# First four attention units: probabilities turned by a product with diagonals of reciprocals, and a product over zeros ahead of each group of turns

## The chip, the cores and the metric

The kernel runs on one core of one Trainium2 chip. The metric is the time of one execution on the device in microseconds (us), lower is better. TensorE (PE) multiplies matrices, VectorE (DVE) and ScalarE (ACT) work on vectors, GpSimd (POOL) does slower vector work, and SyncE (SP) issues most DMAs. Each engine works through its own queue in order; an instruction that waits holds up everything behind it on that engine.

## The reference

Three stages follow one another: attention with a causal mask and a bias from cumulated gates, then two MLP layers.

```python
B, H, S, D = 4, 8, 576, 64
cum = np.cumsum(np.maximum(s, 0.0), axis=-1)
bias = np.minimum(-(cum[..., :, None] - cum[..., None, :]), 0.0)
scores = np.where(causal, -1e9, q @ k.T / 8 + bias)
attn = np.exp(scores - scores.max(-1))
attn = attn / (attn.sum(-1) + 1e-9)
x = (attn @ v)                      # -> 2304 x 512
h = x @ w_in; r = np.maximum(h, 0)  # 512 -> 2048
x = (s * r * r + b) @ w_out         # 2048 -> 512
h = x @ w_in2; g = np.maximum(h, 0) + alpha * np.minimum(h, 0)
x = g @ w_out2
```

## The kernel before

Attention is cut into 32 **units**: a batch, a pair of heads, and a range of query rows. Units 0 to 3 are the four pairs of heads of batch 0, each with query rows 0 to 319 in blocks of 64, 128 and 128 rows. Only after all four does the first token block of the MLP have all of its 512 inputs, so the first MLP product, `hp` on L781, stands behind them. From there on `attention()` yields single steps of the later units in between MLP products, and PE has work of one kind while the other waits.

For one head of a unit, `scores` writes the bias (L433 on DVE for the first head, L429 on ACT for the second), multiplies q and k on PE (L455), adds bias and product and keeps the row's extreme on DVE (L459), takes the exponential with the row's sum on ACT (L471), adds 1e-9 to the sums and takes reciprocals on DVE (L478, L479), and multiplies each block by its reciprocals on POOL (L482). Then `values` turns the blocks on PE into a bank `pt` (L513: six 128x128 turns a head in two banks, each a transpose against the identity), copies the bank to `pf` (L517, ACT for the first bank, DVE for the second), multiplies with v into `av` (L529), and copies the result out (L544).

Besides, the first MLP weights are unpacked: for each half of a packet, `convert` does one pass on ACT (L140) and two on DVE (L141, L142) into `wt_<packet>_<half>`, half 0 from `wi` and half 1 from `wo`; then L130 and L131 split it. The q and k of a unit come by DMA into `nat` and are turned on DVE (L373) into `turned`. `busy(n)` (L97) multiplies zeros into a scratch bank n times on PE; 16 run at the start, and single ones stand between the steps of the first four units.

The code is written per unit, but the order on each engine's queue is set at build time by a scheduler, which moves instructions by its own estimate of when each could start; only `busy` is held in program order. Any change of instructions can therefore move others.

In names such as `probs_0_2_0_508` the parts are batch, pair of heads and range and then a buffer number, and printed names lose digits directly behind letters: `sc_1_0_0_2_0` is the score of block 1 of unit 2, `nm_2_0_1` and `sm_2_0_1` belong to unit 2 (pair 2, range 0), second head. `turned_0_1` and `nat_0_1` are unit 4's (pair 0, range 1), the first that isn't one of the first four.

Of the kernel before, what the change touches and what calls it, by code (L numbers as in the profile page):

```python
# [8 lines left out]
F32 = mybir.dt.float32  # L9
# [4 lines left out]
ALU = mybir.AluOpType  # L14
# [5 lines left out]
def tile_forget_attention__then__two_mlps(  # L20
# [20 lines left out]
    nc = tc.nc  # L41
    B, H, S, D = q.shape
    NT, DM = out.shape
    DFF = w_in1.shape[1] // 2
    P = 128
    NP = H // 2
# [5 lines left out]
    IB = [(0, 64)] + [(64 + 128 * n, 192 + 128 * n) for n in range(4)]  # L52
    R1 = IB[2][1]
    QK = S - R1 + S
    EARLY, NATIVE = NP, 2 * NP

# [8 lines left out]
    one = ctx.enter_context(tc.tile_pool(name="one", bufs=1))  # L67
# [12 lines left out]
    ident = const.tile([P, P], F32, name="ident")  # L80
# [13 lines left out]
    def busy(n):  # L94

        for _ in range(n):
            tc.keep_in_program_order(nc.tensor.matmul(scratch, dense[:, :P], dense, start=True, stop=True))  # L97
# [31 lines left out]
    def split(hi, lo, src, lo_eng=nc.vector):  # L129
        nc.scalar.copy(hi, src)  # L130
        lo_eng.tensor_tensor(out=lo, in0=src, in1=hi.bitcast(F32), op=ALU.subtract)  # L131
# [36 lines left out]
    for f in range(len(SPARE), NF):  # L168
        at = int((f - len(SPARE)) * PACE)
# [106 lines left out]
    class Unit:  # L276
        def __init__(self, n):
            self.n = n
            self.b, self.pr, self.rng = units[n]
            self.tag = "_".join(str(i) for i in units[n])  # L280
            self.h0 = 2 * self.pr
            self.blocks = (0, 1, 2) if self.rng == 0 else (3, 4)
            self.q0, self.q1 = (0, R1) if self.rng == 0 else (R1, S)
            self.nv = 3 if self.rng == 0 else 4
            self.probs = [None, None]

            self.early = 0 < n < EARLY
            self.native = n < NATIVE
            self.n_banks = 0
            self.cums = []  # L290

# [110 lines left out]
    def scores(u, h):  # L402

        own = HALF[h]
        head = u.b * H + u.h0 + h
        flip = u.native and h == 1
        nr = len(u.blocks)
        nm = two.tile([P, 3], F32, tag="nm", name=f"nm_{u.tag}_{h}")
        sm = two.tile([P, 3], F32, tag="sm", name=f"sm_{u.tag}_{h}")
        if u.rng == 0:  # L410
            nc.gpsimd.memset(sm[:, 0:1], 1.0)
        big = None if u.early else two.tile([P, 1088], F32, tag="probs", name=f"probs_{u.tag}_{h}")
        probs, col = {}, 0
        for r in u.blocks:
            i0, i1 = IB[r]
            rows = i1 - i0
            if u.early and r != 1:
                big, col = u.buf(two, 0, F32, "", f"probs{h}{r}"), 0

            width = -(-i1 // P) * P if i1 < S else S  # L420
            pt = probs[r] = big[:, col : col + width]
            col += width
            if width > i1:
                nc.gpsimd.memset(pt[:, i1:], 0.0)
            if r == 0:
                nc.gpsimd.memset(pt[64:P, 0:64], 0.0)

            if flip:
                nc.scalar.activation(  # L429
                    pt[:rows, :i1], u.cums[h][:rows, :i1], AF.Relu, scale=-1.0, bias=cumT[:rows, r, head : head + 1]  # L430
                )
            else:
                nc.vector.tensor_scalar(  # L433
                    out=pt[:rows, :i1], in0=u.cums[h][:rows, :i1], scalar1=cumT[:rows, r, head : head + 1],
                    scalar2=0.0, op0=ALU.subtract, op1=ALU.min,
                )
            nc.gpsimd.affine_select(
                out=pt[:rows, i0:i1], in_=pt[:rows, i0:i1], pattern=[[-1, rows]], base=0,
                channel_multiplier=1, compare_op=ALU.is_ge,
                fill=-MASKED if flip else MASKED,  # L440
            )
        u.probs[h] = probs
        for m, r in enumerate(u.blocks):
            i0, i1 = IB[r]
            rows, n = i1 - i0, i1
            a0 = i0 - u.q0
            pt = probs[r]
            init = -KEEP_ALL if flip else KEEP_ALL
            for j0, j1 in ([(0, n)] if n <= 512 else [(0, 320), (320, n)]):
                sc = u.bank("sc", f"sc{h}_{r}_{j0}")  # L450

                scr, all_ = sc[:rows, : j1 - j0], sc[:, : j1 - j0]
                aq = slice(a0, a0 + P)
                if u.native:
                    nc.tensor.matmul(all_, u.qk[0][own, aq], u.qk[1][own, j0:j1], start=True, stop=True)  # L455
                else:
                    nc.tensor.matmul(all_, u.xs[h][0][:, aq], u.xs[h][1][:, j0:j1], start=True, stop=False)
                    nc.tensor.matmul(all_, u.ql[h][:, aq], u.xs[h][1][:, j0:j1], start=False, stop=True)  # L458
                nc.vector.tensor_tensor_reduce(  # L459
                    out=pt[:rows, j0:j1], in0=scr, in1=pt[:rows, j0:j1], scale=SCALE if flip else -SCALE, scalar=init,  # L460
                    op0=ALU.subtract if flip else ALU.add, op1=ALU.max if flip else ALU.min,
                    accum_out=nm[:rows, m : m + 1],
                )
                if u.n < EARLY:
                    busy(1)
                init = nm[:rows, m : m + 1]
            if flip:
                nc.vector.tensor_scalar(
                    out=nm[:rows, m : m + 1], in0=nm[:rows, m : m + 1], scalar1=-1.0, scalar2=None, op0=ALU.mult
                )  # L470
            nc.scalar.activation(  # L471
                pt[:rows, :n], pt[:rows, :n], AF.Exp, bias=nm[:rows, m : m + 1], scale=1.0 if flip else -1.0,
                accum_out=sm[:rows, m : m + 1],
            )
            yield
        if u.n == 0:
            busy(4)
        nc.vector.tensor_scalar(out=sm[:, :nr], in0=sm[:, :nr], scalar1=1e-9, scalar2=None, op0=ALU.add)  # L478
        nc.vector.reciprocal(sm[:, :nr], sm[:, :nr])  # L479
        for m, r in enumerate(u.blocks):  # L480
            rows, n = IB[r][1] - IB[r][0], IB[r][1]
            nc.gpsimd.tensor_scalar(  # L482
                out=probs[r][:rows, :n], in0=probs[r][:rows, :n], scalar1=sm[:rows, m : m + 1],
                scalar2=1.0, op0=ALU.mult, op1=ALU.mult,
            )
        yield

    def values(u, h):
# [10 lines left out]
        for n_bank, bank in enumerate(banks):  # L499
            f0, fn = bank[0][1], bank[-1][1] + width[bank[-1][0]]  # L500
            tp = u.bank("tr", f"pt{h}_{n_bank}")
            moves = []
            for c, off in bank:
                for r in u.blocks:
                    i0, i1 = IB[r]
                    if P * c >= i1:
                        continue

                    partial = r and P * c > i0
                    o = off + i0 - max(q0, P * c)  # L510
                    moves.append((not partial, -c if partial else o, o, r, min(P * c, S - P)))
            for _, _, o, r, k0 in sorted(moves):
                nc.tensor.transpose(tp[:, o : o + P], u.probs[h][r][:, k0 : k0 + P], ident)  # L513
            n_p = (2 * h + n_bank) % 2
            if u.native:
                pf = two.tile([P, 512], F32, tag=("ph", "pl")[n_p], name=f"pf_{u.tag}_{h}_{n_bank}")
                (nc.scalar.copy, nc.vector.tensor_copy)[n_p](pf[:, f0:fn], tp[:, f0:fn])  # L517
                parts = (pf,)
            else:
                ph = two.tile([P, 512], F32R, tag="ph", name=f"ph_{u.tag}_{h}_{n_bank}")  # L520
                pl = two.tile([P, 512], F32R, tag="pl", name=f"pl_{u.tag}_{h}_{n_bank}")
                split(ph[:, f0:fn], pl[:, f0:fn], tp[:, f0:fn])
                parts = (ph, pl)
            yield
            for z, part in enumerate(parts):
                for c, o in bank:
                    w = width[c]
                    lhs = (u.vn if u.native else u.vs[h])[:, c].rearrange("p z d -> p (z d)")
                    nc.tensor.matmul(  # L529
                        av[:, nq - w : nq], lhs, part[:, o : o + w],  # L530
                        start=(c == 0 and z == 0), stop=(c == last_c and z == len(parts) - 1),
                        skip_group_check=True,
                    )
# [451 lines left out]
    for n in range(len(BLOCKS) * NF):  # L985
# [20 lines left out]
        for j in range(NF):  # L1006
            at = LAG[0] + int((j - len(SPARE)) * PACE) if j >= len(SPARE) else j
# [46 lines left out]
```

## Time and profile before

| | |
|---|---|
| Median of three runs | 1039.33 us (1038.52 to 1040.82) |
| Profiled execution, its own time | 1039.36 us |
| Its span, first to last instruction | 1037.6 us |
| PE busy | 98% of the span |
| DVE / ACT / POOL busy | 65% / 65% / 43% |
| Mean granted TensorE clock | 0.996 |

The span is what the engines' records cover; 1.8 us of the execution lie around it. A row of the timeline tells when an instruction, or a run of like ones, began, how long it took, and in square brackets how long the engine had been idle before and what ended that. Grouped rows give count, busy time and mean.

### The profile page before, as it was taken

How to read it: one execution, taken by the hardware profiler on the slowest of the kernel's cores; microseconds unless marked ns; L12 is line 12 of the kernel's file. 1: busy time of each engine (PE TensorE's matmuls, PEld its weight loads, DVE VectorE, ACT ScalarE, POOL GpSimd, SP SyncE). 2: the span in 40 equal slices, each digit the busy share in tenths (PEclk: the TensorE clock that was granted, in tenths of full speed). 3: DMA queues.
4: the chain of work that ended last, by engine and by line, in shares of the span. 5: the costliest groups of instructions: out<-in, count | busy, mean ns of one | idle time of the engine just before them, and what ended most of it. 6: DMA issues, size and time to landing. Idle time of an engine off the chain costs nothing. (4 is left out here: it accounts for less than half of the span.)

```text
span 1037.6 us, 20643 instructions
## 1 busy us (share of the span) xinstructions
PE 1018.5 (98%) x6949; PEld 925.5 (89%) x6952; DVE 674.4 (65%) x1605; ACT 670.7 (65%) x1668; POOL 450.6 (43%) x876
## 2 busy tenths in 40 slices
PE   9999999999999999999999999999999999999997
PEld 4578899999999999999999888888999999999996
DVE  6899665687677766677655865857665456455443
ACT  5878766777787877878776776645554454445433
POOL 5555675666677576777562000574611011001000
PEclk9899999999999999999999999999999999999999
DMA  7997443343143432324215762645644335334331
GB/s 150 257 249 223 120 76 68 73 98 76 40 89 67 99 72 52 82 65 91 68 34 177 230 199 78 205 148 176 200 154 142 102 114 171 103 102 133 105 102 48
DMA packets 197930, 125.45 MB, mean 121 GB/s; under 512 B 138496, under 2 KB 167936, under 8 KB 197824
## 3 DMA queue, kind: packets, MB, share of 16 engines
q1 hardware_dynamic: 193744, 123.56, 42.8%
q8 instruction: 55, 0.90, 0.4%
q10 hardware_dynamic: 4080, 0.57, 0.3%
q14 instruction: 51, 0.42, 0.1%
HBM read 106.19 MB, written 17.90 MB: 120 GB/s over the span
## 5 line engine op out<-in xcount | busy, mean ns | idle before, releaser
L781 PE MATMUL hp<-xh,w 128*128 128x256 f32 (+1 forms) x1024 | 229.9, 301 | 1.1 <-ACT r L800 1.1
L905 PE MATMUL acc<-w,ring 128*128 128x512 f32 x864 | 214.6, 392 | 1.1 <-DVE ring L131 0.7
L905 PEld LDWEIGHTS acc<-w,ring 128*128 128x128 f32 x864 | 155.9, 188 | 29.4 <-DVE ring L131 1.1
L781 PEld LDWEIGHTS hp<-xh,w 128*128 128x128 f32 x1024 | 171.4, 189 | 9.3 <-ACT r L800 1.4
L895 PE MATMUL acc<-gh,w 128*128 128x256 f32 x896 | 170.3, 286 | 0.4 <-ACT res L924 0.4
L781 PE MATMUL hp<-xl,w 128*128 128x256 f32 (+1 forms) x512 | 152.3, 298 | 0.0
L895 PEld LDWEIGHTS acc<-gh,w 128*128 128x128 f32 x896 | 135.3, 189 | 2.4 <-ACT res L924 1.0
L881 POOL TENSOR_TENSOR cc<-u,t 128x256 f32<-128x256 f32 x32 | 26.9, 839 | 237.2 <-DVE u L872 202.9
L895 PE MATMUL acc<-gl,w 128*128 128x256 f32 x448 | 117.7, 288 | 1.4 <-POOL gl L131 1.4
L482 POOL TENSOR_SCALAR probs<-probs,sm 64x64 f32<-64x64 f32 (+4 forms) x160 | 89.2, 571 | 58.9 <-DVE sm L479 51.9
L471 ACT ACTIVATE probs<-probs,nm 64x64 f32<-64x64 f32 (+4 forms) x160 | 89.9, 562 | 35.8 <-DVE nm L459 26.9
L131 POOL TENSOR_TENSOR gl<-r,gh 128x256 fp32r<-128x256 f32 x112 | 87.7, 784 | 51.3 <-ACT gh L130 41.4
L815 PE MATMUL p<-xs,sums 128*128 128x256 f32 x768 | 104.6, 282 | 0.4 <-DVE u L857 0.4
L815 PEld LDWEIGHTS p<-xs,sums 128*128 128x128 f32 x768 | 98.0, 189 | 2.0 <-DVE u L857 0.6
L781 PEld LDWEIGHTS hp<-xl,w 128*128 128x128 f32 x512 | 97.1, 190 | 2.7
L459 DVE CUSTOM_DVE_ANT_0 probs<-sc,probs 128x320 f32<-128x320 f32 (+3 forms) x160 | 68.4, 428 | 42.1 <-PE sc L458 28.8
L815 PEld LDWEIGHTS p<-xs,w 128*128 128x128 f32 x576 | 79.0, 189 | 8.4 <-DVE u L872 1.7
L800 ACT ACTIVATE r<-hp 128x256 f32<-128x256 f32 (+1 forms) x144 | 58.0, 403 | 43.7 <-PE hp L781 31.6
L815 PE MATMUL p<-xs,w 128*128 128x256 f32 x576 | 82.0, 282 | 2.3 <-DVE u L872 1.5
L895 PEld LDWEIGHTS acc<-gl,w 128*128 128x128 f32 x448 | 79.8, 189 | 2.5 <-POOL gl L131 1.9
L513 PE MATMUL pt<-ident,probs 128*128 128x128 f32 x480 | 75.3, 275 | 3.1 <-POOL probs L482 2.7
L826 DVE SCALAR_TENSOR_TENSOR ph<-pl,misc,ph 128x512 f32<-128x512 f32 x64 | 50.6, 790 | 42.3 <-ACT pl L842 42.3
(151 smaller groups left out, 2104.3 us busy)
## 6 DMA issues: line engine op xcount, KB each, us to landing
sums<-sums_d SPq DMA_DIRECT2D x128, 256.0 KB, 2.7
wi<-in_moe_w_in_dram SPq DMA_DIRECT2D x32, 512.0 KB, 5.0
wo<-in_moe_w_out_dram SPq DMA_DIRECT2D x32, 512.0 KB, 5.1
cum<-cum_d SPq DMA_DIRECT2D x32, 288.0 KB, 3.6
sums_d<-w SPq DMA_DIRECT2D x64, 128.0 KB, 1.9
cum<-cum_d SPq DMA_DIRECT2D x30, 160.0 KB, 3.0
nat<-in_k_dram SPq DMA_DIRECT2D x64, 72.0 KB, 2.5
x_d<-res SPq DMA_DIRECT2D x18, 256.0 KB, 2.4
```

The lines of the kernel that those rows point to most:

```text
L131: lo_eng.tensor_tensor(out=lo, in0=src, in1=hi.bitcast(F32), op=ALU.subtract)
L459: nc.vector.tensor_tensor_reduce(out=pt[:rows, j0:j1], in0=scr, in1=pt[:rows, j0:j1], scale=SCALE if flip else -SCALE, scalar=init, op0=AL ...
L471: nc.scalar.activation(pt[:rows, :n], pt[:rows, :n], AF.Exp, bias=nm[:rows, m : m + 1], scale=1.0 if flip else -1.0, accum_out=sm[:rows, m ...
L482: nc.gpsimd.tensor_scalar(out=probs[r][:rows, :n], in0=probs[r][:rows, :n], scalar1=sm[:rows, m : m + 1], scalar2=1.0, op0=ALU.mult, op1=A ...
L513: nc.tensor.transpose(tp[:, o : o + P], u.probs[h][r][:, k0 : k0 + P], ident)
L781: nc.tensor.matmul(hs, a[:, c], b[c], start=(n == 0), stop=(n == len(terms) * NCC - 1))
L800: relus.append(nc.scalar.activation(r, hs, AF.Relu, scale=1.0 / W_SCALE).ins)
L815: nc.tensor.matmul(bank, lhs[:, c * P : (c + 1) * P], rhs[:, c], start=(start and c == 0 and z == 0), stop=(c == 1 and z == 2), skip_group ...
L826: nc.vector.scalar_tensor_tensor(out=r, in0=u, scalar=nalpha[:, f : f + 1], in1=r, op0=ALU.mult, op1=ALU.add).ins
L881: nc.gpsimd.tensor_tensor(out=cc[:, T:], in0=u3, in1=t5, op=ALU.add)
L895: nc.tensor.matmul(banks[d] if count == 2 else acc[d // 2][:, d % 2], a[:, d * P : (d + 1) * P], b, start=(f == 0 and (d % 2 == 0 or count ...
L905: nc.tensor.matmul(banks[m], a[:, m * P : (m + 1) * P], b, start=(f == 0 and b is woh and a is gh), stop=(f == NF - 1 and a is gl),)
```

## The change

For units 0 to 3 (`SPREAD = 4`) the 24 multiplies on POOL (three a head) are gone. In their place DVE multiplies the identity by the reciprocals, block by block, into a tile `diag` (tags xs0 and xs1): a diagonal matrix of 64x64, 128x128 and 128x128 per head. A turn is no longer a transpose against the identity but a product of the block with its diagonal, which turns and scales at once; it is a product in fp32, and masked columns (`skip`) are left out, so three turns a head have 64 columns and three have 128. Eight memsets of 64x64 on POOL go, and one `busy(1)` is added ahead of each group of turns: two banks, two heads, four units, so 16.

```diff
-    EARLY, NATIVE = NP, 2 * NP
+    EARLY, NATIVE, SPREAD = NP, 2 * NP, 4
...
-            if r == 0:
+            if r == 0 and not u.spread:
                 nc.gpsimd.memset(pt[64:P, 0:64], 0.0)
...
         nc.vector.reciprocal(sm[:, :nr], sm[:, :nr])
+        if u.spread:
+            u.diag[h] = one.tile([P, QK], F32, tag=f"xs{h}", name=f"diag{h}_{u.tag}")
         for m, r in enumerate(u.blocks):
             rows, n = IB[r][1] - IB[r][0], IB[r][1]
+            if u.spread:
+                turn = u.diag[h][:rows, m * P : m * P + rows]
+                nc.vector.tensor_scalar(
+                    out=turn, in0=ident[:rows, :rows], scalar1=sm[:rows, m : m + 1], scalar2=None, op0=ALU.mult
+                )
+                continue
             nc.gpsimd.tensor_scalar(
...
             tp = u.bank("tr", f"pt{h}_{n_bank}")
             moves = []
+            if u.n < EARLY:
+                busy(1)
...
-                    moves.append((not partial, -c if partial else o, o, r, min(P * c, S - P)))
-            for _, _, o, r, k0 in sorted(moves):
+                    moves.append((not partial, -c if partial else o, o, r, min(P * c, S - P), max(0, P * c - i0)))
+            for _, _, o, r, k0, skip in sorted(moves):
+                if u.spread:
+                    rows = IB[r][1] - IB[r][0]
+                    at = (r - u.blocks[0]) * P
+                    nc.tensor.matmul(
+                        tp[:, o + skip : o + rows], u.probs[h][r][:rows, k0 : k0 + P],
+                        u.diag[h][:rows, at + skip : at + rows], start=True, stop=True,
+                    )
+                    continue
                 nc.tensor.transpose(tp[:, o : o + P], u.probs[h][r][:, k0 : k0 + P], ident)
```

In the changed kernel the new multiply is L488, the new turn L528, and the old turn L533; L455, L459, L373, L517, L529 and L781 are L457, L461, L375, L537, L549 and L801.

The scheduler's order moves with it. The queue of SP's DMAs keeps its order, and from the first MLP products on, PE's keeps it too.

On DVE, where unit 2 scores its first head, `sc_1_0_0_2_0` is block 1 and `sc_2_0_0_2_0` block 2. Before:

```order
L459 ISA probs_0_2_0_508,nm_2_0_0_505<-sc_1_0_0_2_0_539,probs_0_2_0_508 128x192
L459 ISA nm_2_0_0_505 128x1
L141 TENSOR_SCALAR wt_1_0_226<-wt_1_0_226 128x512
L459 ISA probs_0_2_0_520,nm_2_0_0_505<-sc_2_0_0_2_0_550,probs_0_2_0_520 128x320
L459 ISA nm_2_0_0_505 128x1
L142 SCALAR_TENSOR_TENSOR wt_1_0_226<-wi_1_216,wt_1_0_226 128x512
```

After:

```order
L141 TENSOR_SCALAR wt_2_0_246<-wt_2_0_246 128x512
L142 SCALAR_TENSOR_TENSOR wt_2_0_246<-wi_2_242,wt_2_0_246 128x512
L141 TENSOR_SCALAR wt_2_1_250<-wt_2_1_250 128x512
L461 ISA probs_0_2_0_512,nm_2_0_0_509<-sc_1_0_0_2_0_543,probs_0_2_0_512 128x192
L461 ISA nm_2_0_0_509 128x1
L142 SCALAR_TENSOR_TENSOR wt_2_1_250<-wo_2_243,wt_2_1_250 128x512
```

The unpacking of packets 1 and 2, which stood behind this score, now stands ahead of it; in the same way block 1 of the second head now stands behind `wt_3_0` and `wt_3_1`.

On DVE, at the turn of unit 4's q and k (`turned_0_1`). Before:

```order
L459 ISA probs_0_3_0_737,nm_3_0_1_722<-sc_2_0_0_3_0_770,probs_0_3_0_737 128x320
L459 ISA nm_3_0_1_722 128x1
L142 SCALAR_TENSOR_TENSOR wt_3_1_649<-wo_3_263,wt_3_1_649 128x512
L468 TENSOR_SCALAR nm_3_0_1_722<-nm_3_0_1_722 128x1
L131 TENSOR_TENSOR xl_0_870<-xf_433,xh_0_869 128x256
L373 STREAM_TRANSPOSE turned_0_1_695<-nat_0_1_564 128x832
```

After:

```order
L461 ISA probs_0_3_0_672,nm_3_0_0_669<-sc_0_0_0_3_0_689,probs_0_3_0_672 64x64
L461 ISA nm_3_0_0_669 64x1
L470 TENSOR_SCALAR nm_2_0_1_588<-nm_2_0_1_588 128x1
L375 STREAM_TRANSPOSE turned_0_1_703<-nat_0_1_570 128x832
L480 TENSOR_SCALAR sm_2_0_1_589<-sm_2_0_1_589 128x3
L435 TENSOR_SCALAR probs_0_1_0_831<-cum_0_0_1_579,cumT 128x448
L537 COPY pf_2_0_0_1_715<-pt_1_0_2_0_712 128x64
L435 TENSOR_SCALAR probs_0_1_0_831<-cum_0_0_1_579,cumT 128x576
L481 RECIPROCAL sm_2_0_1_589<-sm_2_0_1_589 128x3
L461 ISA probs_0_3_0_672,nm_3_0_0_669<-sc_1_0_0_3_0_705,probs_0_3_0_672 128x192
```

It stood behind the last score of unit 3's second head; now it stands behind the first score of unit 3's first head, with the other five scores of unit 3 behind it.

On PE, the last rows ahead of the first MLP product. Before:

```order
L513 MATMUL pt_0_0_3_0_832<-ident,probs_0_3_0_737 128x128 x2
L513 MATMUL pt_1_0_3_0_849<-ident,probs_0_3_0_737 128x128
L455 MATMUL sc_3_0_0_0_1_934<-turned_0_1_695 128x448
L529 MATMUL av_0_3_0_831<-pf_3_0_1_0_838,vn_3_0_223 128x320
L529 MATMUL av_0_3_0_831<-pf_3_0_1_0_838,vn_3_0_223 128x192
L529 MATMUL av_0_3_0_831<-pf_3_0_1_1_851,vn_3_0_223 128x64
L97 LDWEIGHTS dense
L97 MATMUL acc_first_96<-dense 128x512
L781 MATMUL hp_0_0_881<-xh_0_869,w_0_0_0_204 128x256
```

After:

```order
L528 MATMUL pt_0_0_3_0_846<-diag_0_3_0_793,probs_0_3_0_735 128x64 x2
L528 MATMUL pt_0_0_3_0_846<-diag_0_3_0_793,probs_0_3_0_735 128x128
L528 MATMUL pt_0_0_3_0_846<-diag_0_3_0_793,probs_0_3_0_746 128x128 x2
L549 MATMUL av_0_3_0_845<-pf_3_0_1_0_853,vn_3_0_223 128x320
L549 MATMUL av_0_3_0_845<-pf_3_0_1_0_853,vn_3_0_223 128x192
L97 LDWEIGHTS dense
L97 MATMUL acc_first_96<-dense 128x512
L549 MATMUL av_0_3_0_845<-pf_3_0_1_1_867,vn_3_0_223 128x64
L97 LDWEIGHTS dense
L97 MATMUL acc_first_96<-dense 128x512
L801 MATMUL hp_0_0_897<-xh_0_885,w_0_0_0_204 128x256
```

The same first MLP product stands at the end of both; the score `sc_3_0_0_0_1` of unit 4 moved ahead of this group of turns, and a product over zeros came in.

## Rows read from the trace of the kernel before

**Rows 1.** The page: the span, and the engines' busy time, share, instructions.

```profile
span 1037.6 us, 20643 instructions
PE 1018.5 (98%) x6949; PEld 925.5 (89%) x6952; DVE 674.4 (65%) x1605; ACT 670.7 (65%) x1668; POOL 450.6 (43%) x876
```

**Rows 2.** By stretch: length, busy us and count per engine, granted clock, DMA share.

```profile
0.00:60.00 60.00, 54.13 (x227) 30.74 (x230) 46.38 (x154) 40.55 (x117) 34.53 (x113) 0.94 0.86 208
38.00:42.00 4.00, 4.00 (x11) 2.42 (x10) 3.62 (x14) 3.40 (x11) 0.23 (x1) 0.50 0.48 107
48.00:55.00 7.00, 5.64 (x29) 4.06 (x30) 6.97 (x16) 4.91 (x13) 5.04 (x10) 1.00 1.05 334
60.00:120.00 60.00, 59.68 (x392) 50.10 (x391) 53.23 (x112) 49.03 (x119) 35.30 (x52) 1.00 0.80 219
```

**Rows 3.** Timeline of DVE: start, duration, instruction [idle before <-releaser].

```profile
22.48 0.39 DVE L141 TENSOR_SCALAR wt<-wt 128x512 uint32<-128x512 uint32 x1
29.05 0.34 DVE L459 CUSTOM_DVE_ANT_0 probs<-sc,probs 128x192 f32<-128x192 f32 x1
33.14 0.91 DVE L141 TENSOR_SCALAR wt<-wt 128x512 uint32<-128x512 uint32 x1 [0.68 <-ACT wt L140]
48.66 1.03 DVE L373 STREAM_TRANSPOSE turned<-nat 128x832 f32<-128x832 f32 x1
```

**Rows 4.** DMA of wo, packet 2, issued at 29.2 (SP).

```profile
L212 SPq DMA_DIRECT2D wo<-in_moe_w_out_dram x1: 1804/1804/1804, 29.2 to 29.2; - x1
DMA to landing us min/median/max: 7.7/7.7/7.7
```

**Rows 5.** DMA of wo, packet 3, issued at 31.6 (SP).

```profile
L212 SPq DMA_DIRECT2D wo<-in_moe_w_out_dram x1: 503/503/503, 31.6 to 31.6; - x1
DMA to landing us min/median/max: 8.2/8.2/8.2
```

**Rows 6.** DMAs of unit 4's k into nat, issued up to 44.5 (SP).

```profile
L325 SPq DMA_DIRECT2D nat<-in_k_dram x3: 311/496/1033, 42.6 to 44.5; - x3
DMA to landing us min/median/max: 2.9/3.8/3.8
```

**Rows 7.** Timeline of PE.

```profile
15.90 0.82 PE L513 MATMUL pt<-ident,probs 128*128 128x128 f32 x6
33.30 1.06 PE L513 MATMUL pt<-ident,probs 128*128 128x128 f32 x6 [0.70 <-POOL probs L482]
49.97 0.49 PE L513 MATMUL pt<-ident,probs 128*128 128x128 f32 x3
50.39 1.99 PE L455 MATMUL sc<-turned 64*128 64x448 f32 x6
53.79 1.20 PE L529 MATMUL acc_first<-pf,vn 128*128 128x320 f32 x6
54.82 1.03 PE L97 MATMUL acc_first<-dense 128*128 128x512 bf16 x4
58.68 0.47 PE L781 MATMUL hp<-xh,w 128*128 128x256 f32 x1
```

**Rows 8.** Timeline of POOL, the multiplies of one head.

```profile
32.54 1.22 POOL L482 TENSOR_SCALAR probs<-probs,sm 64x64 f32<-64x64 f32 x3 [2.53 <-DVE nm L468]
```

**Rows 9.** Groups of DVE by shape, 8 to 60 us: busy us, mean ns, idle before.

```profile
L459 DVE CUSTOM_DVE_ANT_0 probs<-sc,probs 128x320 f32<-128x320 f32 x9 | 4.3, 476 | 1.0 <-PE sc L455 1.0
L141 DVE TENSOR_SCALAR wt<-wt 128x512 uint32<-128x512 uint32 x8 | 4.3, 535 | 1.9 <-ACT wt L140 1.9
L479 DVE RECIPROCAL sm<-sm 128x3 f32<-128x3 f32 x8 | 1.3, 159 | 0.1
L433 DVE TENSOR_SCALAR probs<-cum,cumT 128x448 f32<-128x448 f32 x1 | 0.4, 437 | 0.0
```

**Rows 10.** Groups of ACT by shape, 8 to 60 us.

```profile
L471 ACT ACTIVATE probs<-probs,nm 128x320 f32<-128x320 f32 x8 | 4.4, 550 | 0.3 <-DVE nm L459 0.3
L471 ACT ACTIVATION_READ_ACCUMULATOR probs<-probs,nm 128x1 f32 x19 | 3.6, 187 | 0.0
```

More of the change, by code (lines that the diff above doesn't have):

```diff
@@ L288, in __init__ @@
             self.native = n < NATIVE
+            self.spread = n < SPREAD
+            self.diag = [None, None]
             self.n_banks = 0
```

## Prediction

> **What bounds the kernel now.** I read the page first: PE is busy for 1018.5 of 1037.6 us [rows 1]. With 2% idle, the question is where the idle time lies, and the stretches answer it. In the first 60 us PE is busy for 54.13, and its clock is 0.94 on average; from 60 to 120 it idles for 0.3 us in all [rows 2]. So from the first MLP product, which starts at 58.68 [rows 7], PE is a queue that is never empty, and whatever delays that product delays all that follows; whatever brings it forward brings the end forward. The case is decided by one number: when that product starts.
>
> Next I read the timeline backwards from it. In 48 to 55 us DVE is busy for 6.97 of 7.00 us and PE for 5.64 [rows 2]: PE waits for what the vector engines hand over. In that stretch DVE turns unit 4's q and k at 48.66 [rows 3]. Their last load is issued at 44.5 and takes up to 3.8 us [rows 6], so it lands near 48.3, and DVE takes it up almost at once. Before the change all scores of units 2 and 3 are behind DVE by then, and 10.0 us later (58.68 less 48.66) the first MLP product starts.
>
> **The change part by part.** *POOL.* The multiplies of one head take 1.22 us in the row that shows three together [rows 8], eight heads some 10 us, all of it gone. POOL is off the chain except where a turn waits for it, as at 33.30 for 0.70 us [rows 7]. The eight memsets I cost at nothing, because the 16 products over zeros at the start cover them; without that cover each is smaller than one of the three multiplies (0.4), so 3.2 in all is their upper bound, as a gain.
>
> *DVE.* Three diagonals a head come in. The trace shows no such row. From below, the reciprocal of 3 columns takes 0.159; from above, a shift of 512 columns 0.39 undisturbed [rows 3, 9]. On the line between the two, 64 columns cost 0.19 and 128 columns 0.22, which makes 0.62 a head and 5.0 for eight (bounds 3.8 and 9.4). I take 5.0, since the sizes lie near the lower end.
>
> In return DVE may run faster. A shift of L141 takes 0.39 at 22.48, but 0.91 at 33.14 while POOL multiplies from 32.54 to 33.76 [rows 3, 8]; the mean of eight is 0.535 [rows 9], so their loss is 8 x 0.145 = 1.2 us, and as much again for the eight passes of L142 (an estimate from the same rows): up to 2.4 back, not all of it owed to these multiplies. The Trainium skill, "SBUF — State Buffer", section "SBUF: two separate sides", states that VectorE in its faster modes and GpSimd take turns at a shared pair of ports, and that the loser is blocked for the whole instruction; the trace agrees with 0.39 against 0.91. By that rule alone, taking POOL's multiplies away speaks for the change, and all of the 2.4 would come back.
>
> *PE.* Six turns in a row take 0.82 and three 0.49, so a turn costs 0.11 [rows 7]. The new turn is an fp32 product as L455 is: 1024 columns in two passes each take 1.99 less about 0.27 of tail, or 0.84 ns a column and pass, so 128 columns take 0.215. For 64 columns I take the same, because the 128 rows of the block must be loaded in any case (lower bound 0.11). That is +0.63 a head, 5.0 for eight (bounds 2.5 and 5.0). A product over zeros costs about 0.215 (four in 1.03 with the next row 0.86 later [rows 7]): 16 cost 3.4. All this matters only where PE isn't waiting; in the first 60 us it idles 5.9 us [rows 2].
>
> *The order.* This term decides. As the queue of the DMAs does not change, unit 4's loads land near 48.3 whatever the engines do. But DVE's queue has changed in two places.
>
> First, block 1 of unit 2's first head, scored at 29.05 before [rows 3], now stands behind the shift of `wt_2_1`, which needs `wo` of packet 2; that landed at 29.2 + 7.7 = 36.9 [rows 4]. Block 1 of its second head stands behind `wt_3_1`, which needs 31.6 + 8.2 = 39.8 [rows 5] and then ACT's and DVE's passes, so about 42. Behind the waiting shift in DVE's queue stand all further scores, and behind those PE's turns and `av`. So heads that were finished at 29 to 46 us are done 8 us later and more, and DVE reaches the turn of unit 4 with five scores of unit 3 undone.
>
> Second, that turn now stands ahead of those five scores, and waits for the load. I start it at 48.66, as before. Then on DVE, one after another: the turn 1.03; sums of unit 2's second head 0.16; bias of 448 columns 0.44; a copy 0.20; bias of 576 columns 0.56 (0.437 x 576/448); reciprocal 0.16; score of block 1 0.34 and its read-out 0.08 [rows 3, 9]; a split `xl` 0.40 and the copy's 0.20 as estimates near the bias row; three diagonals 0.62; score of block 2 0.48 and read-out 0.08. Together 4.55. Then ACT's exponential with its read-out 0.55 + 0.19 = 0.74 [rows 10], sums and reciprocal 0.32, a score that stands between 0.42, two diagonals 0.41 and a handoff of 0.1: 1.99. PE gets the diagonals of unit 3's first head at 48.66 + 4.55 + 1.99 = 55.2.
>
> From there PE has, in its new order up to the first MLP product: 12 turns x 0.215 = 2.6; scores of unit 4, 448 + 320 + 256 + 448 columns in two passes at 0.84 ns = 2.5; three groups of `av` at 1.03 = 3.1 (the group at 53.79 is followed at 54.82 [rows 7]); 12 products over zeros x 0.215 = 2.6; and one wait for ACT's copy of a bank, some 0.8 by the row of 0.55. Sum 11.6, so the product starts at **66.8** instead of 58.68, +8.1 us. Working it with the bounds of turn (64 columns at 0.11: -0.6) and diagonal (0.48 to 1.17 a head: -0.2 to +0.9) and the load 0.4 earlier gives +7 to +9.
>
> *What is given back later.* PE's order does not change afterwards, and it idles 0.3 us in 60 to 120, while DVE is busy for 53.23 of 60 [rows 2], and stays as late as PE makes it. I take nothing, and bound it at 3 us, for weights that would be waited for less. The sum: 1039.36 + 8.1 = 1047.5, and as the profiled execution lies on the median (1039.33), 1047.4.
>
> **The rivals.** *Faster.* The order is harmless, because DVE and PE arrive earlier than the weights' DMAs let me assume. Then each head's own chain is shorter by 1.22 - 0.62 = 0.6 on its last step, and the 2.4 of slowed DVE passes come back in the stretch where DVE is busy throughout: 1039.3 - 3.0 = 1036.3. For it: PE's waits ahead of turns are for POOL [rows 7]. Against it: the fp32 turns and zeros add 8.4 us to PE against 5.9 idle, and the scores do stand behind the weights in the queue. The rule of the page cited above is the one that would carry this. Chance 0.14.
>
> *No change.* DVE is never long without work, so what it does in another order adds up to the same; then +5.0 for diagonals, -2.4 for undisturbed passes and -2 to -3 of DVE's waits filled gives 1039 to 1040. Against it: in an in-order queue the waits at `wt_2_1` and `wt_3_1` are not filled. Chance 0.10.
>
> *Slower still.* The clock falls in the new gap. Before, it stands at 0.50 from 38 to 42 us [rows 2], which is the 1.2 of the two levels of 1.2 and 2.4 GHz; the mean of 0.94 over 60 us means some 7 us at half. With PE waiting more in 42 to 55, as much of that may fall on the 11.6 us of PE's own chain, where it costs half of 7.2, 3.6 us: 1051. The zeros ahead of the turns speak against it, as they are queued behind the same waits. Chance 0.15.
>
> *That the change doesn't do what it says* would be a turn that still waits as long for DVE's diagonals as for POOL; this is part of my likeliest case and needs no price of its own.
>
> **How the numbers follow.** About 0.2%, or 2 us, is what a measurement of this kernel can tell from no change. Likeliest, with 0.61: +8.1, 1047.4, between 1044.5 (3 us given back) and 1048.5. With 0.15 about 1051, with 0.10 about 1039.5, with 0.14 about 1036.3. The range from 1039 to 1052 leaves out the faster rival and little else. Faster 0.14, same 0.10, slower 0.61 + 0.15 = 0.76.
>
> **What would show it.** After the change, the first MLP product near 66.8 us, later ones all 7 to 9 us late with the same spacing; unit 2's block 1 scored after 37 us on DVE with a long wait on the `wt` shifts ahead of it; PE idle for some 8 to 12 us more in the first 60; L141 without values near 0.9 where POOL multiplied. Step by step: diagonals at 0.19 to 0.22, new turns 0.215 apart, zeros 0.215 each. I am wrong if the first MLP product starts before 60 us: then the scores did not wait for the weights as their order says, or the zeros and fp32 turns were idle time. I am also wrong if it starts late but the delay melts away before 300 us; then PE's full share hid waits that the records count as work.

## The result and the profile after

The changed kernel took 1047.49 us (median of six runs, 1046.51 to 1049.31) against 1040.39 for the kernel before in the same session, a ratio of 1.0081 with an interval from 1.0065 to 1.0097. It is slower by about 8 us.

The runs of one kernel differ in how long TensorE's clock stands at half, so a few comparisons below name the mean granted clock. At 0.995 to 0.997, eight runs of the changed kernel from all sessions have a median of 1046.56 and 29 runs of the kernel before 1038.49: 8.1 us.

The page of the changed kernel, from a run of 1049.31 us at a clock of 0.991 (span and busy time, to be held against [rows 1]):

```profile
span 1047.5 us, 20756 instructions
PE 1031.1 (98%) x7012; PEld 934.9 (89%) x7016; DVE 674.0 (64%) x1629; ACT 671.7 (64%) x1668; POOL 437.9 (42%) x844
```

Its stretches, as in [rows 2]:

```profile
0.00:60.00 60.00, 56.55 (x234) 32.37 (x237) 42.48 (x157) 35.43 (x101) 20.75 (x78) 0.86 0.84 205
60.00:120.00 60.00, 59.27 (x377) 48.53 (x377) 50.36 (x119) 47.74 (x116) 31.10 (x45) 1.00 0.69 192
```

PE is busier in the first 60 us (56.55 against 54.13), DVE less busy (42.48 against 46.38) and POOL much less (20.75 against 34.53). The clock is 0.86 there against 0.94, and the first MLP product, at 58.68 before, starts at 70.22. That run isn't on the clock of the profile before, so the readings below come from a later run of the same kernel that is (`after_third`, 1046.57 us at 0.996). The same stretch there, and the DVE and PE timelines around unit 4's turn:

```profile
0.00:60.00 60.00, 54.13 (x247) 32.40 (x251) 44.71 (x167) 37.15 (x107) 20.85 (x78) 0.94 0.86 206
44.00:65.00 21.00, 20.64 (x104) 13.62 (x106) 14.79 (x63) 14.07 (x42) 3.79 (x8) 1.00 0.99 247
```

```profile
47.41 1.05 DVE L375 STREAM_TRANSPOSE turned<-nat 128x832 f32<-128x832 f32 x1 [1.65 <-DMA nat<-in_k_dram]
...
49.27 0.45 DVE L435 TENSOR_SCALAR probs<-cum,cumT 128x448 f32<-128x448 f32 x1 [0.77 <-DMA cum<-cum_d]
...
53.41 0.63 DVE L488 TENSOR_SCALAR diag<-ident,sm 64x64 f32<-64x64 f32 x3
```

```profile
44.30 1.80 PE L528 MATMUL pt<-diag,probs 128*128 128x64 f32 x12 [1.08 <-DVE diag L488]
...
51.63 1.73 PE L528 MATMUL pt<-diag,probs 128*128 128x64 f32 x12
53.28 0.80 PE L457 MATMUL sc<-turnedk,turnedq 64*128 64x320 f32 x2
54.02 1.66 PE L528 MATMUL pt<-diag,probs 128*128 128x64 f32 x10
55.61 1.55 PE L457 MATMUL sc<-turned 64*128 64x448 f32 x4
...
63.72 1.56 PE L528 MATMUL pt<-diag,probs 128*128 128x64 f32 x10
65.95 1.13 PE L549 MATMUL av<-pf,vn 128*128 128x320 f32 x4 [0.68 <-ACT pf L537]
...
67.33 0.47 PE L801 MATMUL hp<-xh,w 128*128 128x256 f32 x1
```

Up to the first MLP product PE's time is, in the kernel before and then in `after_third`:

```profile
0.00:58.68 58.68, 52.81 (x217) 29.47 (x221) 46.00 (x152) 39.43 (x113) 33.21 (x111) 0.94 0.87 210
0.00:67.33 67.33, 60.79 (x280) 37.02 (x285) 48.10 (x178) 40.55 (x115) 23.46 (x81) 0.95 0.84 208
```

At an equal clock the first MLP product starts at 67.33 against 58.68 [rows 7], 8.6 us later. The turn of unit 4 does wait for its load, 1.65 us, with DVE's queue behind it, and the diagonals of unit 3's first head are done at 53.41 + 0.56 = 53.97 (the next DVE instruction starts then). PE takes them up at 54.02. But PE came to that place without a gap: from 44.3 on it has no wait of its own until 65.95. DVE's late diagonals and PE's longer queue arrive at the same moment. Of the 8.6 us PE is busy for 8.0 (60.79 less 52.81) and idle for 0.7 (6.54 less 5.87): the loss is work that the old waits did not hide. Whether the new order kept those waits from being filled, or the work alone makes the loss, the trace can't say by itself.

### The profile page after: what moved, and what is told of

It is laid out like the page before. It is cut to its first block, busy times and chain, and to the rows that moved or that the text cites. A ratio compares the mean times of both kernels' runs of the same rounds, so it can differ in the third digit from the quotient of the medians.

```text
span 1047.5 us, 20756 instructions
## 1 busy us (share of the span) xinstructions
PE 1031.1 (98%) x7012; PEld 934.9 (89%) x7016; DVE 674.0 (64%) x1629; ACT 671.7 (64%) x1668; POOL 437.9 (42%) x844
## 5 line engine op out<-in xcount | busy, mean ns | idle before, releaser
L801 PE MATMUL hp<-xh,w 128*128 128x256 f32 (+1 forms) x1024 | 229.9, 301 | 1.1 <-ACT r L820 1.1
L801 PEld LDWEIGHTS hp<-xh,w 128*128 128x128 f32 x1024 | 171.4, 189 | 9.4 <-ACT r L820 1.5
L801 PE MATMUL hp<-xl,w 128*128 128x256 f32 (+1 forms) x512 | 152.3, 298 | 0.0
L461 DVE CUSTOM_DVE_ANT_0 probs<-sc,probs 128x320 f32<-128x320 f32 (+3 forms) x160 | 68.3, 428 | 49.6 <-PE sc L460 28.5
L801 PEld LDWEIGHTS hp<-xl,w 128*128 128x128 f32 x512 | 97.1, 190 | 2.7
L492 POOL TENSOR_SCALAR probs<-probs,sm 128x448 f32<-128x448 f32 (+4 forms) x136 | 77.1, 580 | 40.3 <-DVE sm L481 39.3
L567 DVE TENSOR_TENSOR xf<-av,xf 64x128 f32<-64x128 f32 (+3 forms) x88 | 28.0, 319 | 69.4 <-ACT xf L566 68.9
```

The lines of the kernel that those rows point to most:

```text
L461: nc.vector.tensor_tensor_reduce(out=pt[:rows, j0:j1], in0=scr, in1=pt[:rows, j0:j1], scale=SCALE if flip else -SCALE, scalar=init, op0=AL ...
L492: nc.gpsimd.tensor_scalar(out=probs[r][:rows, :n], in0=probs[r][:rows, :n], scalar1=sm[:rows, m : m + 1], scalar2=1.0, op0=ALU.mult, op1=A ...
L567: nc.vector.tensor_tensor(out=dst, in0=src, in1=dst, op=ALU.add)
L801: nc.tensor.matmul(hs, a[:, c], b[c], start=(n == 0), stop=(n == len(terms) * NCC - 1))
```

## The experiments

The theories: **order** (DVE's new order delays the first four units, as predicted), **work** (PE simply has more to do, with fp32 turns and zeros), and **clock** (the half-clock stretch became longer). Each kernel's first MLP product is given beside its time, since the first 60 us can be read there free of what later units do. The queues are held by `issue_after`, which puts instructions behind a given one on the same engine.

### The changed kernel again: `after_again`, `after_third`, `after_fourth`

> The changed kernel once more, for a second profile. Its first profile granted 0.86 of the clock in the first 60 us and had PE busy without a gap from 38 to 68 us. Order theory (DVE's queue delays units 2 and 3 behind the weights and unit 4's loads): with more clock PE idles 4 us or more in 36 to 60, and the first MLP product still starts near 66 to 68 us. Work theory (PE has about 8.4 us more to do, the fp32 turns and the zeros): PE stays busy without gaps there and the first product comes near 67 to 70. Clock theory (the longer stretch at half clock makes the loss): the first product comes before 63 us where the clock is not lower than in the kernel before.

> The changed kernel for another profile, wanted at a mean clock near 0.996 as in four of its ten runs so far. Theory that PE's own added work bounds the first 60 us: PE without gaps over 0.3 us from 36 to 56, first MLP product 65 to 68 us. Theory that DVE's order bounds it: PE waits 2 us or more there for DVE's diagonals or scores, first product 66 to 68 us.

> As after_third, in case that one falls on the lower clock of 0.991 again: at that clock the first MLP product at 70 to 70.5 us and PE without gaps from 38 to 68.

`after_again` took 1047.73 us (ratio 1.0080, 1.0053 to 1.0106); its profile fell on 0.991 again, first product at 70.42. The other two fell on 0.996: 1046.57 and 1046.55, first products at 67.33 and 66.78. Four runs at 0.991 have a median of 1049.36, 2.8 us over those at 0.995 to 0.997. So the clock explains those 2.8 us, and not the 8 that stay at the equal clock. Order and work are both still possible: PE's waits in 36 to 56 are 1.5 us in `after_third`, between what the two theories asked for.

### The order without the work: `order_only`

The kernel before, with DVE's queue as after the change: unit 2's block 1 and 2 behind the shifts and merges of packets 2 and 3, five of unit 3's scores behind unit 4's turn. For this the unpacking of packet 3 also moves, in the code, ahead of the scores of unit 2's second head (not in the cut shown).

```diff
+    def queued(n, h, m):
+        key = None
+        if n == 2 and m:
+            key = ((0, 2, 1), 'shift' if m == 1 else 'or') if h == 0 else ((0, 3, 1), 'or')
+        if n == 3 and (h or m):
+            key = 'turned', 4
+        return tc.issue_after(marks[key]) if key else nullcontext()
...
+                with queued(u.n, h, m):
+                    nc.vector.tensor_tensor_reduce(
```

> The kernel before, with its instructions queued on DVE in the order of the changed one at the two places: unit 2's scores behind the weights of packets 2 and 3, unit 4's turn ahead of five of unit 3's scores. No diagonals, no zeros. Order theory: 5 to 9 us slower than before, 1045 to 1049, first MLP product at 64 to 68 us. Work theory and clock theory: within 2 us of before, as it adds no work.

Measured: 1043.49 us, ratio 1.0039 (1.0026 to 1.0053), six runs all at 0.991. In its profile:

```profile
44.35 0.90 PE L524 MATMUL pt<-ident,probs 128*128 128x128 f32 x3 [6.07 <-POOL probs L493]
...
68.67 0.47 PE L792 MATMUL hp<-xh,w 128*128 128x256 f32 x1
```

```profile
0.00:60.00 60.00, 49.91 (x182) 26.38 (x186) 40.32 (x137) 35.45 (x101) 32.44 (x110) 0.86 0.86 211
44.00:60.00 16.00, 15.43 (x42) 8.65 (x44) 7.32 (x29) 7.46 (x24) 7.02 (x18) 0.56 0.93 240
```

Without any added work the first product is off by 10 us, but not at an equal clock: PE waits 6.07 us at one place, and from 41 to 58 us the clock stands at half (0.56 in 44 to 60), which makes 17.1 us of the first 100 against 6.8 in the kernel before. The 10.3 us more at half are worth up to 5.1 us of PE's time, an estimate from these two numbers, so about half of the 10 goes with the clock; all six runs have this clock, and no run shows the order without it. The end is later by only 4.9 us: by the tenth part of the MLP's `hp` products it is 9 us late, by three tenths 5.2. So the order alone is costly, and half of it is given back here, where PE had taken up turns of unit 4 ahead of the first product and then waits less (0.8 us from 60 to 300, against 3.3 before).

### The work without the order: `work_only`

All of the change, but packets 2 and 3 unpacked behind unit 2's and unit 3's scores, and unit 4's turn and biases behind unit 3's scores and first diagonals. The DMAs of the first weights are issued where they were.

```diff
-        packet(0, 2)
+        fetch(0, 2)
...
-        packet(0, 3)
-        yield from alternate(scores(us[3], 0), values(us[2], 0), transpose_qk(u))
+        with tc.issue_after(marks[2, 1, 2]):
+            packet(0, 2)
+        yield from alternate(scores(us[3], 0), values(us[2], 0))
         yield from alternate(scores(us[3], 1), values(us[2], 1))
+        with tc.issue_after(marks[3, 1, 1]):
+            packet(0, 3)
+        with tc.issue_after(marks["diag", 3, 0]), tc.issue_after(marks[3, 1, 2]):
+            for _ in transpose_qk(u):
+                pass
```

> The changed kernel with all its diagonals, fp32 turns and zeros, but with packets 2 and 3 unpacked behind unit 2's and unit 3's scores, and unit 4's q and k turned behind all of unit 3's scores, as in the kernel before. Order theory: 1039 to 1042. Work theory: 1046 to 1048, as the changed kernel. Clock theory: as the changed kernel where the clock is as low.

Measured: 1045.93 us, ratio 1.0066 (1.0048 to 1.0085); the three runs at 0.995 to 0.997 took 1043.42 to 1044.00. First product, in a run at 0.995:

```profile
64.86 0.47 PE L810 MATMUL hp<-xh,w 128*128 128x256 f32 x1
```

With these two places put back 6.2 of the 8.6 us at the first product stay, and 5.4 of the 8.1 at the end. This falls between the expectations, much nearer to work than to order. The queues are near those of the kernel before but not the same: the packets stand behind all of unit 2's scores, and two of the products over zeros (0.2 us each) come only after the first MLP product.

### Which of the two places: `turn_back` and `weights_back`

`turn_back` is `work_only` with the packets left as in the changed kernel, so that only unit 4's turn and biases go back. `weights_back` is `work_only` with unit 4's turn left as in the changed kernel, so that only the packets go back.

> The changed kernel, zeros and fp32 turns included, with only unit 4's turn and biases put back behind unit 3's scores; unit 2's scores still stand behind packets 2 and 3. At a granted clock of 0.995 to 0.997 the changed kernel took 1045.6 to 1047.7 and work_only 1043.4 to 1044.0. If unit 4's turn is the costly place: 1043 to 1044.5 at that clock. If the weights are: 1045.5 to 1047, no gain.

> The changed kernel, zeros and fp32 turns included, with only packets 2 and 3 put back behind unit 2's and unit 3's scores; unit 4's turn stays ahead of five of unit 3's scores. If unit 4's turn is the costly place: 1045.5 to 1047 at a clock of 0.995 to 0.997. If the weights are: 1043 to 1044.5.

`turn_back` took 1043.73 us (ratio 1.0047, 1.0030 to 1.0064), and its seven runs at 0.995 to 0.997 have a median of 1043.26, 3.3 under the changed kernel's and no worse than `work_only`. `weights_back` took 1050.88 (ratio 1.0101, 1.0068 to 1.0133), more than the changed kernel. First `turn_back`, then `weights_back` on DVE, then on PE:

```profile
65.22 0.47 PE L807 MATMUL hp<-xh,w 128*128 128x256 f32 x1
```

```profile
47.84 1.05 DVE L375 STREAM_TRANSPOSE turned<-nat 128x832 f32<-128x832 f32 x1 [3.35 <-DMA cum<-cum_d]
```

```profile
51.84 2.08 PE L552 MATMUL acc_first<-pf,vn 128*128 128x320 f32 x4 [5.14 <-ACT pf L540]
...
72.36 0.47 PE L807 MATMUL hp<-xh,w 128*128 128x256 f32 x1
```

Of the two places the costly one is unit 4's turn. Unpacking the weights ahead of unit 2's scores costs nothing that can be seen. On the contrary: where the packets went back and the turn did not, DVE came to the turn sooner and stood before it for 3.35 us (1.65 in the changed kernel), with the rest of its queue behind it, and PE waited 5.14 us. In the changed kernel the weights' passes seem to fill a part of that wait.

### Turns and zeros apart: `turns_only`, `dve_scale`, `zeros_only`, `no_zeros`, `no_zeros_late`

`turns_only` is `work_only` without the 16 zeros. `dve_scale` has the same order and no zeros, but instead of diagonals DVE multiplies the probabilities in place and the old one-pass turns stay. They differ in the turns and in what DVE multiplies.

```diff
             if u.n < EARLY:
-                busy(1)
+                busy(0)
```

```diff
-    EARLY, NATIVE, SPREAD = NP, 2 * NP, 4
+    EARLY, NATIVE, SPREAD = NP, 2 * NP, 0
...
-            nc.gpsimd.tensor_scalar(
+            marks["diag", u.n, h] = (nc.vector if u.n < EARLY else nc.gpsimd).tensor_scalar(
                 out=probs[r][:rows, :n], in0=probs[r][:rows, :n], scalar1=sm[:rows, m : m + 1],
```

> The changed kernel without zeros and with the order of the kernel before (as in work_only): only the diagonals and the fp32 turns are left of the change. Work theory: work_only took 1045.9, so 3 to 5 less, 1041 to 1043; what stays over before is the turns' own PE time. Order theory: 1038 to 1040, no loss left.

> The kernel before with the multiplies of units 0 to 3 moved from POOL to DVE, in place, the old one-pass turns kept, no zeros; order as in work_only. DVE has the multiplies as an addition, PE nothing. Work theory (PE's added turns and zeros cost): 1037 to 1039.5. If instead DVE is what the first 60 us are bound by: 1041 to 1045.

`turns_only` took 1045.68 us (ratio 1.0081, 1.0052 to 1.0109, four runs from 1042.87 at a clock of 0.996 to 1050.46 at 0.989; too few and too far apart for its end time to carry much). `dve_scale` took 1039.26 (ratio 1.0014, 1.0000 to 1.0029), as fast as the kernel before. Their profiles are at 0.996 and 0.995 and have the clock at half for 6.8 us of the first 100, as the profile before has. `turns_only`, then `dve_scale`:

```profile
62.30 0.47 PE L810 MATMUL hp<-xh,w 128*128 128x256 f32 x1
```

```profile
58.52 0.47 PE L810 MATMUL hp<-xh,w 128*128 128x256 f32 x1
```

The pair shows that the fp32 turns, with the diagonals in place of multiplies on DVE, put the first product off by 3.8 us (up to it PE is busy for 58.69 against 51.88 us and idle for 3.6 against 6.6); the two profiles of the changed kernel at one clock differ by 0.55 there, which is the measure of such a difference. The zeros, `work_only` less `turns_only`, come to 64.86 - 62.30 = 2.6. And freeing POOL of the multiplies by giving them to DVE is worth nothing: up to the first product PE's turns wait 4.3 us for DVE's multiplies, where before they waited 2.7 us for POOL's, and the product starts at the same time.

`zeros_only` is the kernel before with the 16 zeros and the old turns and multiplies (`SPREAD = 0` in `work_only`):

> The kernel before with the 16 zeros and nothing else, packets 2 and 3 and unit 4's turn kept behind unit 3's scores as before. Work theory: 2.5 to 4 us slower than before, 1041 to 1043. Order theory: within 1.5 us of before, as PE idled 5.9 us in the first 60 and the zeros fit there.

It took 1043.22 us (ratio 1.0052, 1.0037 to 1.0067). The first product is at 58.79, where it was, and yet the end is 4.7 us later, a little more than either theory expected. In its profile:

```profile
0.00:60.00 60.00, 54.12 (x241) 30.47 (x246) 41.54 (x155) 40.98 (x118) 37.13 (x113) 0.97 0.86 209
```

PE idles 5.9 us in the first 60, as in the kernel before [rows 2], so the zeros did not fill its waits. The clock stands at half for only 3.4 us there against 6.8, which is worth up to 1.7 us (an estimate from these numbers) and hides a part of what the zeros add; the run doesn't decide between the theories. After the first product PE waits more, 5.3 us from 60 to 300 against 3.3; the order of the later units differs from the kernel before, and the rest of the loss stays open. So the end times of kernels with an order of their own carry an uncertainty of some microseconds, and I give more weight to the first products.

`no_zeros` is the changed kernel without the zeros, its order left to the scheduler; in `no_zeros_late` DVE is held to the changed kernel's order by the code of `order_only`.

> The changed kernel without its 16 added products over zeros. The scheduler moves other things too: unit 4's turn goes back behind four of unit 3's six scores, and unit 2's first block 1 ahead of packet 2's weights. Work theory: 16 x 0.215 = 3.4 us less, some 1044. Order theory: most of the loss goes with the order, 1040 to 1042. Clock theory: without the zeros the clock stays at half for longer, 1048 to 1050.

> The changed kernel without its 16 added zeros, but with the changed kernel's order on DVE at both places (unit 2's scores behind packets 2 and 3, unit 4's turn ahead of five of unit 3's scores). Without zeros and with a freer order the kernel took 1041.5. Theory that the zeros cost by their order: 1045 to 1047, as the order is here and the zeros are not. Theory that the zeros cost by their own PE time: 1041 to 1042.5, as without zeros.

`no_zeros` took 1041.51 us (ratio 1.0028, 1.0012 to 1.0043); its first product is at 68.83 in a profile at 0.989 that has the clock at half for 20.5 of the first 100 us, so it can't be held against the others. `no_zeros_late` took 1055.37 (ratio 1.0178, 1.0150 to 1.0207), worse than either theory said. In `no_zeros_late`:

```profile
48.74 2.00 PE L539 MATMUL pt<-diag,probs 128*128 128x64 f32 x6 [4.64 <-DVE diag L499]
...
78.28 0.47 PE L812 MATMUL hp<-xh,w 128*128 128x256 f32 x1
```

```profile
36.00:60.00 24.00, 19.20 (x69) 12.05 (x69) 16.93 (x64) 14.11 (x40) 4.95 (x10) 0.76 0.95 227
60.00:120.00 60.00, 59.78 (x346) 47.09 (x348) 43.67 (x108) 41.98 (x103) 24.96 (x38) 0.95 0.63 167
```

Here PE waits 4.64 us for a diagonal and the clock is then at 0.76 in 36 to 60 and 0.95 in 60 to 120: it stands at half for 27.3 of the first 100 us, in two stretches, the second from 48 to 66. The two kernels differ by 14 us, all of it from the order and what follows from it. Against the changed kernel, which has that order and the zeros, the kernel without them is 8 us slower: in this order the zeros save more than they take. What part of these microseconds is the waits and what the clock, the runs can't separate.

## Why the prediction was right, point by point

**The time** was forecast at 1047.4 and came out at 1047.49, and the first MLP product, forecast at 66.8, started at 67.33 and 66.78 in the two profiles at the clock of the kernel before. Not every step behind the number held, and that it came out so close is luck: the waiting that I counted on was not there, and work that I held to be hidden was as long.

**Decided at the first product, nothing given back.** Right. The product is 8.6 us late in `after_third` and the span ends at 1044.8 against 1037.6, 7.2 later; 1.4 are given back, within the bound of 3.

**Unit 4's loads set DVE's time.** Right in kind. DVE was ready 1.65 us before the loads were there, as the sentence on the waiting turn had it, and `turn_back` and `weights_back` show its place as the costly one of the two. I started the turn at 48.66, it started at 47.41; on the other hand I had no wait for the gates of unit 4's bias (0.77, the row at 49.27). The sum on DVE from the turn to the diagonals was 6.5, measured 53.97 - 47.41 = 6.6.

**The weights' places.** Wrong. I held it for a cause that unit 2's scores stand behind `wt_2_1` and `wt_3_1`. They do, and block 1 is scored at 37.86, after 37 as forecast, but the wait ahead of it is not long. In `after_third`:

```profile
37.51 0.43 DVE L141 TENSOR_SCALAR wt<-wt 128x512 uint32<-128x512 uint32 x1 [0.68 <-ACT wt L140]
37.86 0.35 DVE L461 CUSTOM_DVE_ANT_0 probs<-sc,probs 128x192 f32<-128x192 f32 x1
```

And `turn_back`, which keeps that place, is as fast as `work_only`, which undoes it. The step failed because I asked only what the scores wait for, and not when their results are wanted; all of it is ready before unit 4's loads are.

**PE's queue from the diagonals to the product.** Forecast 11.6, measured 67.33 - 54.02 = 13.3. The term that was too small is the turn: five take 55.61 - 54.02 = 1.59, so 0.32 each and not 0.215 (a single one, from 59.09 to 59.35, 0.26), and twelve cost about 1.1 us more than I had; the four scores of unit 4 were 0.6 over my rule of columns. This error and the earlier start of unit 4's turn nearly cancel. The weight loads of the new turns, in `after_third`:

```profile
L528 PEld LDWEIGHTS pt<-diag,probs 128*128 128x128 f32 x80 | 11.6, 199 | 7.7 <-issue 2.9 <-ACT w L130 2.0 <-DVE pf L537 1.0
...
L528 PEld LDWEIGHTS pt<-diag,probs 64*128 64x128 f32 x16 | 2.6, 200 | 0.6
```

A pass of 64 or of 128 columns goes with a load of 0.2, and a turn with two of them, so leaving out masked columns saved nothing that shows. The Trainium skill, "TensorE: Matmul & The Clock Gate", section "Step-by-step: what each phase is for", states that a weight load's time goes by its columns and not by its rows; the trace agrees, with 199 ns for 128 rows and 200 for 64.

**Diagonals.** Forecast 5.0 in all with bounds 3.8 and 9.4; in `after_third` 16 take 5.0 and 8 take 2.1, 7.1 together, inside the bounds but 2.1 over the forecast. Undisturbed they came as expected (0.63 a head at 53.41); beside a pass of POOL three took 1.70 in the first profile of the changed kernel:

```profile
37.47 1.70 DVE L488 TENSOR_SCALAR diag<-ident,sm 64x64 f32<-64x64 f32 x3
```

```profile
37.71 1.39 POOL L131 TENSOR_TENSOR w<-wt,w 128x512 fp32r<-128x512 f32 x1 [2.46 <-DVE w L131]
```

**DVE faster without POOL's multiplies.** The size was right, the cause mostly not. `after_third` has

```profile
L141 DVE TENSOR_SCALAR wt<-wt 128x512 uint32<-128x512 uint32 x8 | 4.0, 497 | 3.0 <-ACT wt L140 3.0
...
L142 DVE SCALAR_TENSOR_TENSOR wt<-wi,wt 128x512 uint32<-128x512 uint32 x4 | 2.8, 688 | 0.0
L142 DVE SCALAR_TENSOR_TENSOR wt<-wo,wt 128x512 uint32<-128x512 uint32 x4 | 2.7, 681 | 0.0
```

In the kernel before, the groups of L142 read:

```profile
L142 DVE SCALAR_TENSOR_TENSOR wt<-wo,wt 128x512 uint32<-128x512 uint32 x4 | 3.7, 925 | 0.0
L142 DVE SCALAR_TENSOR_TENSOR wt<-wi,wt 128x512 uint32<-128x512 uint32 x4 | 3.6, 906 | 0.0
```

L141's mean went from 0.535 [rows 9] to 0.497, that of L142 from 0.92 to 0.68, which is 8 x 0.04 + 8 x 0.23 = 2.2 us, near the 2.4 I had as the most; the larger part came from L142, which I had only estimated. But in the kernel before L142's mean was raised by two long passes, of 1.57 and 1.66 us, and both began beside a split of weights on POOL and not beside a multiply. The first of them:

```profile
37.20 1.57 DVE L142 SCALAR_TENSOR_TENSOR wt<-wi,wt 128x512 uint32<-128x512 uint32 x1
```

```profile
36.96 1.27 POOL L131 TENSOR_TENSOR w<-wt,w 128x512 fp32r<-128x512 f32 x1
```

The changed kernel has these splits too, and there the diagonals meet them (1.70 beside 1.39): what L142 gained, the diagonals lost. The Trainium skill's rule of the shared ports ("SBUF — State Buffer", section "SBUF: two separate sides"), cited ahead of the result, agrees with both pairs, 1.57 beside 1.27 and 1.70 beside 1.39. What faster passes would have brought was not on the path: `dve_scale` has POOL free of the multiplies and is as fast as before.

**What makes up the loss.** This I had wrong in its weights. I called the order the term that decides, with 8 to 12 us more of idle time on PE in the first 60, and held the 8.4 us of turns and zeros to be hidden in idle time for a part. In `after_third` PE idles 5.9 us in the first 60, as before, and up to the first product it is busy 8.0 us longer. At the first product, at equal clock, it comes to 3.8 for the fp32 turns (`turns_only` less `dve_scale`), 2.6 for the zeros (`work_only` less `turns_only`) and 67.33 or 66.78 less 64.86, about 2.2, for the order, together 8.6. The spans of the same four profiles, 1037.6, 1041.0, 1042.2 and 1044.8, give 3.4, 1.2 and 2.6. Each step rests on one or two profiles a side, and both times the turns are the largest part. The parts don't add up by themselves, though: the order alone costs 10 us at the first product (`order_only`, up to 5 of it by the clock), and little on top of the work, because DVE's wait and PE's longer queue run side by side.

**Rivals.** *Slower still* came in its time, not in its mechanism: four of twelve runs of the changed kernel are at a clock of 0.991 and end 2.8 us later, where I had 3.6, but in the two profiles of that kind the half-clock stretches lie from 11 to 21 and from 31 to 38 us, and not in a new gap from 42 to 55. *No change* and *faster* fell with `dve_scale` and `turns_only`: the room on DVE and POOL was there and was worth nothing.

## What to carry to other kernels

When two engines are near a tie, a prediction can hit the time with the wrong weights: price both queues up to the handoff, and ask which one still arrives late if the other is put right. A small edit in a scheduled kernel may move something elsewhere, here a transpose that waits for a DMA, ahead of work that was ready; what stands behind a wait on the same engine pays for it. A scaling folded into a turn isn't free when it makes a one-pass turn a two-pass product with a weight load for each pass.

## What was not expected of the hardware

The same kernel has its half-clock stretch at different places from run to run: in the first 100 us the changed kernel had it for 17.1 us in two profiles and for 6.8 in two, with 2.8 us between the ends. In `order_only`, `weights_back` and `no_zeros_late` a stretch at half begins within PE's wait of 4.6 to 6.1 us and goes on after it (0.56 in 44 to 60 in the first), so that the time at half came on top of the wait. That the wait brought it is argued from its place and not shown: the changed kernel's stretch from 11 to 21 us has no such wait ahead of it.
